# Moving 9 KB instead of 6 KB of each first row of wq, and spreading the moved rows over seven DMA engines

## The chip, the cores and the metric

The kernel runs on one core of a Trainium2 chip. A core has five compute or control engines, which the profile calls PE (TensorE, matmuls), PEld (its weight loads), DVE (VectorE), ACT (ScalarE), POOL (GpSimd) and SP (SyncE), each with its own stream of instructions, and 16 DMA engines, which carry every transfer between HBM and the on-chip memory SBUF (128 partitions). The metric is the device time of one execution in microseconds (us); the median of three runs before the change is 1315.1 us (1315.02 to 1315.15).

## The reference

One decoding step for two sequences, all in float32: a layer norm, attention of 32 query heads over a cache of 8 key/value heads with 32768 positions, an output projection, and beside it a gated MLP whose output, through a SiLU, multiplies the attention's.

```python
xn = _layernorm(x)                               # x: (2, 1, 512)
q = (xn @ wq).reshape(2, 1, 32, 128)             # wq: (512, 4096)
scores = einsum("bhqd,bhkd->bhqk", q, k) * 128 ** -0.5   # k, v: (2, 8, 32768, 128), each for 4 heads
s = (softmax(scores) @ v) @ wo                   # wo: (4096, 512)
gate, up = xn @ W_gate, xn @ W_up                # (512, 1792)
g = silu((gate * (gate > 0) * up) @ W_down)      # (1792, 512)
return x + s * g
```

The caches are 2 x 268 MB, the weights some 28 MB; everything is read once.

## The kernel before

**Staging.** SBUF holds a ring of three slots of 64 KB a partition (`SLOTS`, `SLOT` = 16384 floats). Each K or V load fills a slot: 128 partitions x 64 KB, 8 MB; for each of the 16 (sequence, KV head) groups there are two K and two V tiles. SP issues all large loads, in the order of the program (`load`, L72), and waits before each until its slot is free. DVE turns a K tile in 32 x 32 blocks in place (`turn_part`, L357), PE makes the scores (`score`, L370), then follow the maximum, the exponentials on ACT (L421), a permuting matmul (L424) and the product with V (`values`, L445). For the last two groups (L509 to L527) the order is written out by hand so that the last V tile is consumed right after it has landed. At the end the output projection `wo` comes in pieces of falling size (L533), and its products (L545, L556) end the program.

**The start.** The ring's three slots first hold weights: `wqs` (wq), `gus` (gate and up) and `wds` (W_down). The rows of wq are dealt so that partition p holds rows 4p to 4p+3; the *first row* of a partition is row 4p. wq would fill its slot with 64 KB a partition. It doesn't: the first `SHIFT` = 1536 floats (6 KB) of each of the 128 first rows are left out of the large load (L81) and are brought by loads of their own into the free end of W_down's slot (`moved`, L82). These loads have 20 rows each (`SET` = 4 x `SPREAD`, `SPREAD` = 5), arranged as 5 x 4 over the partitions, six times, and one each of 5 and of 3 rows (`REST`). They are issued from SP ahead of gate (five of them) and behind it (three), L105 to L115. `moved` has 64 partitions and `NT` = 4 columns of SHIFT floats; POOL sets it to zero beforehand (L91), since not every place is filled.

**q.** `project_q` (L224) multiplies the normed x with wq: `products(half, part)` makes chunks of 512 columns, first from `wqs` (k below `NKC` = 4), then from `moved` (k from 4 on, with `xnx`, the matching entries of x brought into the same places by small DVE copies and a transpose, L158 to L180). Two copies `qs` (L257), 8 small matmuls (L260), `turned` (L268), four matmuls with `spread` (L270) and eight copies (L281) then bring q into `qt`, which the scores read.

**The MLP.** After `project_q` come `mlp_gu(0)` and `mlp_gu(1)` (L292), `mlp_h` (L305 to L310) and `mlp_down` (L318). The calls are at L477 to L481; PE executes in this order. The slot of wq is taken by `k_0_0` when the products from `wqs` are done, that of gate and up by `k_0_1` after `mlp_gu(1)`, that of W_down and `moved` by `v_0_0` after `mlp_down` and the moved products.

**POOL** makes constants at the start: `ident`, then `qt`, `place` and others set to zero (L120 to L131), `spread` (L184), `same` (L197), `perm` (L205). It issues no DMA.

Of the kernel before, what the change touches and what calls it, by code (L numbers as in the profile page):

```python
# [8 lines left out]
F32 = mybir.dt.float32  # L9
# [4 lines left out]
P = 128  # L14
Q = 32
# [4 lines left out]
TK = P * ROWS  # L20
SLOTS = 3
ALIGN = 512
SHIFT = 1536
SPREAD = 5
WO_PIECES = (16, 8, 4, 2, 1, 1)
WO_WIDE = 28

# [2 lines left out]
def kernel(  # L30
# [12 lines left out]
    nc = tc.nc  # L43
    B, HKV, SK, DH = kc.shape
    D = x.shape[2]
# [5 lines left out]
    NKC = D // P  # L51
    FC = F // 4
    FI = F // P
# [6 lines left out]
    const = ctx.enter_context(tc.tile_pool(name="const", bufs=1))  # L60
# [7 lines left out]
    def slot(name):  # L68
        return ring.tile([P, SLOT], F32, tag="r", align_bytes=ALIGN, name=name)

    def load(dst, src):
        nc.sync.dma_start(dst, src)  # L72

    wqs, gus, wds = slot("wq"), slot("gu"), slot("wd")
    QN = wq.shape[1]
    HP = P // 2
    SET = 4 * SPREAD
    FULL = P // SET
    REST = [(FULL * SET, SPREAD), (FULL * SET + SPREAD, P - FULL * SET - SPREAD)]
    NT = FULL // 2 + 1  # L80
    load(wqs[:, : SLOT - SHIFT], wq.rearrange("(p i) n -> p (i n)", p=P)[:, SHIFT:])  # L81
    moved = wds[:HP, FI * D : FI * D + NT * SHIFT].rearrange("p (t n) -> p t n", t=NT)  # L82

    row = work.tile([P, 512], F32, tag="row", name="xp", bufs=3)
    xp = row[:32, :]
# [8 lines left out]
    def load_gu(w, src):  # L94
        load(
            gus[:, w * NKC * F : (w + 1) * NKC * F],
            src.rearrange("(p i) f -> p (i f)", p=P),
        )

    first_rows = wq.rearrange("(p i) n -> p i n", i=NKC)[:, 0, :SHIFT]  # L100

    def place_of(k):
        return slice(Q * (k % 2), Q * (k % 2) + SET), k // 2

    for k in range(FULL + len(REST)):  # L105
        if k == 5:
            load_gu(0, wg)
        part, t = place_of(k)
        if k < FULL:
            rows = first_rows[k * SET : (k + 1) * SET, :]  # L110
            load(moved[part, t, :], rows.rearrange("(b a) n -> a b n", b=4))
        else:
            at, n = REST[k - FULL]
            dst = moved[part, t, :].rearrange("(a b) n -> a b n", b=4)[:n, 0, :]
            load(dst, first_rows[at : at + n, :])  # L115
    load_gu(1, wu)
    load(wds[:, : FI * D], wd.rearrange("(p i) d -> p (i d)", p=P))
    wdt = wds[:, : FI * D].rearrange("p (i d) -> p i d", i=FI)
# [2 lines left out]
    make_identity(nc, ident)  # L121
    eps_t = const.tile([32, 1], F32, name="eps_t")
    nc.gpsimd.memset(eps_t, EPS)
    qt = const.tile([P, NG, 4, Q], F32, name="qt")
    nc.gpsimd.memset(qt, 0.0)
    place = const.tile([P, 2 * P], F32, name="place")
# [13 lines left out]
    m_ps = ps_c.tile([P, 512], F32, name="m_ps")  # L140
# [6 lines left out]
    xc, sq = xc_row[:32, :], sq_row[:32, :]  # L147
# [6 lines left out]
    nc.vector.reciprocal(st[:, 4:5], st[:, 3:4])  # L154
    nc.vector.tensor_scalar(xc, xc, st[:, 4:5], None, op0=ALU.mult)  # L155
    xnp = const.tile([P, NKC, 32], F32, name="xnp")
    xnx = const.tile([HP, NT, 32], F32, name="xnx")
    nc.vector.memset(sq, 0.0)  # L158
    xfirst = xc.rearrange("m (p i) -> m i p", i=NKC)[:, 0, :]
    for k in range(FULL + len(REST)):  # L160
        to = sq[:, k * Q : k * Q + SET].rearrange("m (a b) -> m a b", b=4)
        if k < FULL:
            cols = xfirst[:, k * SET : (k + 1) * SET]
            nc.vector.tensor_copy(to, cols.rearrange("m (b a) -> m a b", b=4))
        else:
            at, n = REST[k - FULL]
            nc.vector.tensor_copy(to[:, :n, 0], xfirst[:, at : at + n])
    xcol = xc.rearrange("b (p i) -> b i p", i=NKC)
    for i in range(NKC):
        nc.tensor.transpose(m_ps[:, i * 32 : (i + 1) * 32], xcol[:, i, :], ident[:32, :32])  # L170
    for t in range(NT):
        nc.tensor.transpose(
            m_ps[:HP, (NKC + t) * 32 : (NKC + t + 1) * 32],
            sq[:, t * HP : (t + 1) * HP],
            ident[:32, :32],
        )
    nc.vector.tensor_copy(xnp.rearrange("p k m -> p (k m)"), m_ps[:, : NKC * 32])
    nc.vector.tensor_copy(
        xnx.rearrange("p k m -> p (k m)"), m_ps[:HP, NKC * 32 : (NKC + NT) * 32]
    )  # L180

    spread = work.tile([P, 4, 4, Q], F32, tag="row", name="spread", bufs=3)
# [12 lines left out]
    n = 1  # L195
# [5 lines left out]
    for s in range(NS):  # L201
        dst = perm[:, s, :].rearrange("p (k z c h) -> p z k c h", k=4, z=2, h=REP)[:, s]
# [21 lines left out]
    def project_q():  # L224
        pick = ident.rearrange("p (c m) -> p c m", c=4)[:, :, :B]
        nq = 2 * REP * 4 * B
        def products(half, part):
            pq = S[0][half]
            for k in part:
                for c in range(4):  # L230
                    n0 = (half * 4 + c) * 512
                    cut = min(512, max(0, SHIFT - n0))
                    last = NKC + NT - 1 if cut else NKC - 1
                    i = NKC - 1 - k
                    at = cut if i == 0 else 0
                    if k < NKC and at < 512:
                        lo = i * QN + n0 - SHIFT
                        lhs, rhs, a, b = xnp[:, i, :], wqs[:, lo + at : lo + 512], at, 512
                    elif k >= NKC and cut:
                        t = k - NKC  # L240
                        lhs, rhs, a, b = xnx[:, t, :], moved[:, t, n0 : n0 + cut], 0, cut
                    else:
                        continue
                    nc.tensor.matmul(  # L244
                        pq[32 * c : 32 * c + 32, a:b],
                        lhs,
                        rhs,
                        start=(k == 0),
                        stop=(k == last),
                    )  # L250

        for part in (range(NKC), range(NKC, NKC + NT)):
            for half in range(2):
                products(half, part)
        for half in range(2):
            qs = work.tile([P, 512], F32, tag="row", name=f"qs_{half}", bufs=3)
            nc.vector.tensor_copy(qs, S[0][half])  # L257
            for h in range(REP):
                lo = (half * REP + h) * 4 * B
                nc.tensor.matmul(  # L260
                    m_ps[:, lo : lo + 4 * B],
                    qs[:, h * DH : (h + 1) * DH],
                    pick,
                    start=True,
                    stop=True,
                )
        turned = const.tile([P, nq], F32, name="turned")
        nc.vector.tensor_copy(turned, m_ps[:, :nq])  # L268
        for e in range(4):
            nc.tensor.matmul(  # L270
                pt_ps[:, e * nq : (e + 1) * nq],
                spread[:, e].rearrange("p k l -> p (k l)"),
                turned,
                start=True,
                stop=True,
            )
        qp = pt_ps[:, : 4 * nq].rearrange("p (e f h m) -> p f m e h", e=4, f=2, h=REP)
        for half in range(2):
            for kb in range(4):
                part = slice(Q * kb, Q * kb + Q)  # L280
                nc.vector.tensor_copy(  # L281
                    qt[part, half * 8 : half * 8 + 8, :, kb * REP : (kb + 1) * REP],
                    qp[part, half],
                )
# [18 lines left out]
    def mlp_h():  # L303
        g, u = gu_sb[0], gu_sb[1]
        nc.vector.scalar_tensor_tensor(  # L305
            g[:, :FC], g[:, :FC], 0.0, g[:, :FC], op0=ALU.is_gt, op1=ALU.mult
        )
        nc.vector.tensor_mul(g[:, :FC], g[:, :FC], u[:, :FC])
        ht = work.tile([P, FI, 32], F32, tag="row", name="ht", bufs=3)
        nc.vector.transpose(  # L310
            ht.rearrange("p i m -> p (i m)"), g[:, :FC].rearrange("p (f i) -> p i f", i=FI)
        )
        return ht

    def mlp_down(ht):
        for i in range(FI):
            a = i % 4
            nc.tensor.matmul(  # L318
                m_ps[32 * a : 32 * a + 32, :],
                ht[:, i, :],  # L320
                wdt[:, i, :],
                start=(i < 4),
                stop=(i >= FI - 4),
            )
        part = work.tile([P, 512], F32, tag="row", name="down", bufs=3)
        nc.vector.tensor_copy(part, m_ps)
        for c in range(4):
            nc.tensor.matmul(
                pt_ps[32 * c : 32 * c + 32, :P],
                fold,  # L330
                part[:, c * P : (c + 1) * P],
                start=True,
                stop=True,
            )
        nc.scalar.activation(gy, pt_ps[:, :P], AF.Silu)
# [117 lines left out]
    def finish_group(g):  # L453
# [11 lines left out]
        if b == B - 1:  # L465
            src = OS.pop(hk).rearrange("p b c (q i) -> p q (b c) i", q=4)
            for dq in range(4):
# [6 lines left out]
                    stop=(hk == HKV - 1 and dq == 3),  # L474
                )

    project_q()  # L477
    mlp_gu(0)
    mlp_gu(1)
    ht = mlp_h()  # L480
    mlp_down(ht)  # L481

    def load_k(g, u):
# [47 lines left out]
    i = 0  # L531
    for n in WO_PIECES:
        load(wos[:, i * D : (i + n) * D], worows[:, i * D : (i + n) * D])  # L533
# [20 lines left out]
    for i in range(WO_WIDE):  # L554
        a = i % 4
# [7 lines left out]
    part = work.tile([P, 512], F32, tag="row", name="wide", bufs=3)  # L563
# [49 lines left out]
```

## Time and profile before

| | before |
|---|---|
| median of 3 runs | 1315.1 us |
| the profiled execution: its own time | 1316.29 us |
| the profiled execution: span, first to last instruction | 1313.4 us |
| bytes read from HBM | 564.67 MB |
| rate over the span | 430 GB/s |
| PE busy | 705.6 us, 54% |
| DVE busy | 657.4 us, 50% |
| POOL busy | 11.9 us, 1% |
| granted TensorE clock, mean | 0.763 |

The span is what the profile's views cover; times in them count from its start. The DMA view, asked for a window, counts the packets that started in it and how many were "under 512 B". A load puts one packet per partition row on an engine, and behind its last one a packet of 4 bytes that reports the engine's share as done; the windows view gives for a stretch each engine's busy time, the granted clock, and the DMA engines' busy share and rate. The views don't number the DMA engines.

### The profile page before, as it was taken

How to read it: one execution, taken by the hardware profiler on the slowest of the kernel's cores; microseconds unless marked ns; L12 is line 12 of the kernel's file. 1: busy time of each engine (PE TensorE's matmuls, PEld its weight loads, DVE VectorE, ACT ScalarE, POOL GpSimd, SP SyncE). 2: the span in 40 equal slices, each digit the busy share in tenths (PEclk: the TensorE clock that was granted, in tenths of full speed). 3: DMA queues.
4: the chain of work that ended last, by engine and by line, in shares of the span. 5: the costliest groups of instructions: out<-in, count | busy, mean ns of one | idle time of the engine just before them, and what ended most of it. 6: DMA issues, size and time to landing. Idle time of an engine off the chain costs nothing.

```text
span 1313.4 us, 10129 instructions
## 1 busy us (share of the span) xinstructions
PE 705.6 (54%) x4678; PEld 198.6 (15%) x4678; DVE 657.4 (50%) x276; ACT 49.9 (4%) x133; POOL 11.9 (1%) x30
## 2 busy tenths in 40 slices
PE   3626357473645547364574636546363654726676
PEld 1201012020111102111121101111011111201121
DVE  2274471917547192653719256281835629177710
ACT  0000000000000000000000000000000000000000
POOL 3000000000000000000000000000000000000000
PEclk9757778776777867677786678879577877957798
DMA  9999999999999999999999999999999999999998
GB/s 403 444 430 434 440 434 428 438 426 441 440 426 436 430 434 438 438 425 438 430 434 441 430 430 436 430 440 436 427 438 432 432 434 438 430 438 428 422 425 353
DMA packets 11059, 565.31 MB, mean 430 GB/s; under 512 B 1280, under 2 KB 1288, under 8 KB 1802
## 3 DMA queue, kind: packets, MB, share of 16 engines
q1 hardware_dynamic: 10974, 564.67, 99.4%
q8 instruction: 36, 0.59, 0.2%
q14 instruction: 5, 0.04, 0.0%
q10 hardware_dynamic: 44, 0.01, 0.0%
HBM read 564.67 MB, written 0.00 MB: 430 GB/s over the span
## 4 chain that ended last, share of the span: by engine, by line
DMA 47%; DVE 26%; PE 25%; issue 1%; ACT 0%; SPq 0%; DVEq 0%; ACTq 0%
DMA k<-in_A_k_cache_dram 41%; DVE k L357 21%; PE o_ps L445 8%; PE s L370 7%; PE pt_ps L424 7%; DMA wo<-in_A_wo_dram 3%; DVE mx L382 3%; DVE pt L428 2%; DMA wq<-in_A_wq_dram 2%; DMA wd<-in_A_wq_dram 1%; PE s L292 1%; PE m_ps L432 0%; PE m_ps L411 0%; ACT w L421 0%; PE m_ps L400 0%
## 5 line engine op out<-in xcount | busy, mean ns | idle before, releaser
L357 DVE STREAM_TRANSPOSE k<-k 128x8192 f32<-128x8192 f32 (+2 forms) x52 | 554.8, 10672 | 136.4 <-DMA k<-in_A_k_cache_dram 136.4
L370 PE MATMUL s<-k,qt 128*32 128x512 f32 x2048 | 301.7, 749 | 479.6 <-DVE k L357 479.6
L445 PE MATMUL o_ps<-v,pt 128*16 128x512 f32 x2048 | 231.0, 609 | 7.0 <-DMA v<-in_A_v_cache_dram 7.0
L370 PEld LDWEIGHTS s<-k,qt 128*32 128x32 f32 x2048 | 71.7, 134 | 703.9 <-DVE k L357 519.1
L457 DVE SCALAR_TENSOR_TENSOR os<-o_ps,rl,mask 128x512 f32<-128x512 f32 x16 | 12.0, 750 | 226.5 <-PE o_ps L445 226.5
L424 PE MATMUL pt_ps<-w,perm 128*128 128x512 f32 x128 | 99.8, 923 | 32.7 <-ACT w L421 18.3
L421 ACT ACTIVATE w<-s,nb 128x512 f32<-128x512 f32 x64 | 43.3, 685 | 1158.2 <-DVE nb L415 1153.2
L382 DVE TENSOR_REDUCE mx<-s 128x2 f32<-128x1024 f32 x32 | 38.6, 1206 | 97.2 <-PE s L370 97.2
L445 PEld LDWEIGHTS o_ps<-v,pt 128*16 128x16 f32 x2048 | 58.2, 99 | 165.9 <-issue 156.8
L428 DVE STREAM_TRANSPOSE pt<-pt_ps 128x512 f32<-128x512 f32 x32 | 22.9, 717 | 111.9 <-PE pt_ps L424 111.9
L424 PEld LDWEIGHTS pt_ps<-w,perm 128*128 128x128 f32 x128 | 31.0, 267 | 80.7 <-issue 48.0
L469 PE MATMUL ot_ps<-os,place 128*128 128x256 f32 x64 | 16.0, 392 | 7.0 <-DVE os L457 7.0
L400 PE MATMUL m_ps<-ident,m 128*1 128x128 f32 x16 | 4.3, 270 | 24.2 <-DVE m L399 24.2
L432 PE MATMUL m_ps<-l,same 128*128 128x1 f32 x32 | 6.7, 280 | 13.5 <-DVE l L431 13.5
L469 PEld LDWEIGHTS ot_ps<-os,place 128*128 128x128 f32 x64 | 11.5, 189 | 15.6 <-DVE os L457 14.4
L421 ACT ACTIVATION_READ_ACCUMULATOR w<-s,nb 128x1 f32 x64 | 12.8, 200 | 0.0
L257 DVE COPY qs<-s 128x512 f32<-128x512 f32 x2 | 1.3, 685 | 20.7 <-PE s L244 20.7
L244 PE MATMUL s<-wq,xnp 128*32 128x512 f32 x58 | 8.7, 714 | 4.5 <-DMA wq<-in_A_wq_dram 4.5
L411 PE MATMUL m_ps<-negs,mrow 1*128 1x1 f32 x32 | 6.4, 267 | 8.3 <-DVE mrow L408 8.3
L432 PEld LDWEIGHTS m_ps<-l,same 128*128 128x128 f32 x32 | 5.4, 210 | 35.7 <-DVE l L431 35.7
L170 PE MATMUL m_ps<-ident,xc 32*128 32x32 f32 x4 | 0.7, 300 | 14.9 <-DVE xc L155 14.9
L556 PE MATMUL s<-wo,ot 128*2 128x512 f32 x56 | 6.6, 592 | 3.3 <-DMA wo<-in_A_wo_dram 3.3
(81 smaller groups left out, 95.8 us busy)
## 6 DMA issues: line engine op xcount, KB each, us to landing
v<-in_A_v_cache_dram SPq DMA_DIRECT2D x2, 4096.0 KB
wq<-in_A_wq_dram SPq DMA_DIRECT2D x1, 7424.0 KB
wo<-in_A_wo_dram SPq DMA_DIRECT2D x1, 4096.0 KB
gu<-in_B_W_gate_dram SPq DMA_DIRECT2D x1, 3584.0 KB
gu<-in_B_W_up_dram SPq DMA_DIRECT2D x1, 3584.0 KB
wd<-in_B_W_down_dram SPq DMA_DIRECT2D x1, 3584.0 KB
wo<-in_A_wo_dram SPq DMA_DIRECT2D x1, 2048.0 KB
wo<-in_A_wo_dram SPq DMA_DIRECT2D x1, 1024.0 KB
```

The lines of the kernel that those rows point to most:

```text
L244: nc.tensor.matmul(pq[32 * c : 32 * c + 32, a:b], lhs, rhs, start=(k == 0), stop=(k == last),)
L292: nc.tensor.matmul(ps[32 * c : 32 * c + 32, :FC], xnp[:, i, :], gut[:, w, i, c * FC : (c + 1) * FC], start=(i == 0), stop=(i == NKC - 1),)
L357: nc.vector.transpose(KT[t][:, part], KT[t][:, part])
L370: nc.tensor.matmul(S[u][s][Q * c : Q * c + Q, :], qt[:, g, e, :], mov[:, s, c, e], start=(e == 0), stop=(e == 3),)
L382: nc.vector.reduce_max(MX[g][:, u * NS : (u + 1) * NS], SB[u], axis=AX.X)
L421: nc.scalar.activation(w, S[u][s], AF.Exp, bias=nb, scale=SCALE, accum_out=LS[g][:, i : i + 1])
L424: nc.tensor.matmul(pt_ps, perm[:, s, :], w, start=(s == 0), stop=(s == NS - 1))
L428: nc.vector.transpose(pt.rearrange("p j m -> p (j m)"), pt_ps)
L432: nc.tensor.matmul(m_ps[:, 300:301], same.rearrange("p r h -> p (r h)"), l, start=True, stop=True)
L445: nc.tensor.matmul(o_ps[Q * a : Q * a + NC * REP], w[:, j, s * NC * REP : (s + 1) * NC * REP], v[:, s, j], start=(u == 0 and s == 0 and j ...
L457: nc.vector.scalar_tensor_tensor(OS[hk][:, b], o_ps, RL.pop(g), mask.unsqueeze(2).to_broadcast([P, NC, DH]), op0=ALU.mult, op1=ALU.mult,)
L469: nc.tensor.matmul(ot_ps.rearrange("p b c i -> p (b c) i"), place[:, lo : lo + P], src[:, dq], start=(hk == 0 and dq == 0), stop=(hk == HK ...
```

## The change

- `SHIFT` becomes 2304 floats: 9 KB of each first row leave the large load.
- The first 80 of the 128 moved rows go, as before, in loads of 20 from SP (four of them, `SETS`), over five DMA engines.
- The other 48 rows go in six loads from GpSimd (`PAIRS`), 8 rows each: four rows into one of the partitions 28 to 31, 60 and 61, four into one of 64 to 67, 96 and 97. Before, between and after them GpSimd issues small loads of x into a tile that nothing reads (`step_over`): 7 partitions, then 14 between the pairs, then 7. They have 2 x 16 bytes a partition.
- `moved` now has all 128 partitions and stays at four columns: 128 x 9216 floats. The copies that place x for it (L160) follow, and `xnx` has 128 partitions.
- gate is loaded second, ahead of all moved rows; up and W_down follow the four sets.
- `project_q` becomes two steps: PE makes the products from `wqs`, then those of gate and up, and only then the moved products and the rest of `project_q`, before `mlp_down`.

```diff
-SHIFT = 1536
+SHIFT = 2304
 SPREAD = 5
+SETS = 4
+PAIRS = 6
...
-    HP = P // 2
     SET = 4 * SPREAD
-    FULL = P // SET
-    REST = [(FULL * SET, SPREAD), (FULL * SET + SPREAD, P - FULL * SET - SPREAD)]
-    NT = FULL // 2 + 1
+    NT = (P - SETS * SET) // (2 * PAIRS)
+    PAIR = 2 * NT
+    LOW, HIGH, UNDER = 28, 64, 7
     load(wqs[:, : SLOT - SHIFT], wq.rearrange("(p i) n -> p (i n)", p=P)[:, SHIFT:])
-    moved = wds[:HP, FI * D : FI * D + NT * SHIFT].rearrange("p (t n) -> p t n", t=NT)
+    moved = wds[:, FI * D : FI * D + NT * SHIFT].rearrange("p (t n) -> p t n", t=NT)
...
-    for k in range(FULL + len(REST)):
-        if k == 5:
-            load_gu(0, wg)
+    load_gu(0, wg)
+    for k in range(SETS):
         part, t = place_of(k)
-        if k < FULL:
-            rows = first_rows[k * SET : (k + 1) * SET, :]
-            load(moved[part, t, :], rows.rearrange("(b a) n -> a b n", b=4))
-        else:
-            at, n = REST[k - FULL]
-            dst = moved[part, t, :].rearrange("(a b) n -> a b n", b=4)[:n, 0, :]
-            load(dst, first_rows[at : at + n, :])
+        rows = first_rows[k * SET : (k + 1) * SET, :]
+        load(moved[part, t, :], rows.rearrange("(b a) n -> a b n", b=4))
     load_gu(1, wu)
...
+    aside = const.tile([P, 64], F32, name="aside")
+
+    def step_over(n, m):
+        view = x[0, 0, : n * 32].rearrange("(p w) -> p w", p=n)[:, :16]
+        view = view.rearrange("p (u n) -> p u n", u=2)[:, :, :4]
+        to = aside[:n, m * 8 : m * 8 + 8].rearrange("p (u n) -> p u n", u=2)
+        nc.gpsimd.dma_start(to, view)
+
+    def pair_rows(m):
+        at = SETS * SET + m * PAIR
+        return slice(at, at + PAIR)
+
+    def low_of(m):
+        return LOW + Q * (m // 4) + m % 4
+
+    step_over(UNDER, 0)
+    for m in range(PAIRS):
+        lo = low_of(m)
+        nc.gpsimd.dma_start(
+            moved[lo : lo + HIGH - LOW + 1 : HIGH - LOW],
+            first_rows[pair_rows(m), :].rearrange("(t a) n -> a t n", a=2),
+        )
+        step_over(14 if m < PAIRS - 1 else 7, m + 1)
...
-        for part in (range(NKC), range(NKC, NKC + NT)):
-            for half in range(2):
-                products(half, part)
+        for half in range(2):
+            products(half, range(NKC))
+        yield
+        for half in range(2):
+            products(half, range(NKC, NKC + NT))
...
-    project_q()
+    steps = project_q()
+    next(steps)
     mlp_gu(0)
     mlp_gu(1)
     ht = mlp_h()
+    for _ in steps:
+        pass
     mlp_down(ht)
```

More of the change, by code (lines that the diff above doesn't have):

```diff
@@ L156 @@
     xnp = const.tile([P, NKC, 32], F32, name="xnp")
-    xnx = const.tile([HP, NT, 32], F32, name="xnx")
+    xnx = const.tile([P, NT, 32], F32, name="xnx")
     nc.vector.memset(sq, 0.0)
     xfirst = xc.rearrange("m (p i) -> m i p", i=NKC)[:, 0, :]
[L160 to L167, printed above, removed]
+    sqt = sq.rearrange("m (t p) -> m t p", t=NT)
+    for k in range(SETS):
+        part, t = place_of(k)
+        nc.vector.tensor_copy(
+            sqt[:, t, part].rearrange("m (a b) -> m a b", b=4),
+            xfirst[:, k * SET : (k + 1) * SET].rearrange("m (b a) -> m a b", b=4),
+        )
+    for m in range(PAIRS):
+        lo = low_of(m)
+        nc.vector.tensor_copy(
+            sqt[:, :, lo : lo + HIGH - LOW + 1 : HIGH - LOW],
+            xfirst[:, pair_rows(m)].rearrange("m (t a) -> m t a", a=2),
+        )
     xcol = xc.rearrange("b (p i) -> b i p", i=NKC)
@@ L172 @@
         nc.tensor.transpose(
-            m_ps[:HP, (NKC + t) * 32 : (NKC + t + 1) * 32],
-            sq[:, t * HP : (t + 1) * HP],
+            m_ps[:, (NKC + t) * 32 : (NKC + t + 1) * 32],
+            sqt[:, t, :],
             ident[:32, :32],
@@ L178 @@
     nc.vector.tensor_copy(
-        xnx.rearrange("p k m -> p (k m)"), m_ps[:HP, NKC * 32 : (NKC + NT) * 32]
+        xnx.rearrange("p k m -> p (k m)"), m_ps[:, NKC * 32 : (NKC + NT) * 32]
     )
```

## The prediction

> **What bounds the kernel now.** I read the page first: the DMA row, the queues, the chain.
>
> ```profile
> span 1313.4 us, 10129 instructions
> DMA  9999999999999999999999999999999999999998
> q1 hardware_dynamic: 10974, 564.67, 99.4%
> q8 instruction: 36, 0.59, 0.2%
> ```
>
> The 16 DMA engines are busy from end to end, almost wholly with the loads of SP's queue; all the caches and weights pass through once, and the change moves none away. The chain of waits in order of time, for the last 150 us, says what the end hangs on:
>
> ```profile
> 1199.27 32.87 DMA k<-in_A_k_cache_dram
> 1232.17 17.32 DVE k L357 x2
> 1263.14 45.24 DMA wo<-in_A_wo_dram
> 1308.43 0.62 PE s L545 x16
> ```
>
> The last weights land at 1308.4 and later, and what follows is a tail of 5 us that the change doesn't touch. A load is complete when the slowest of its engines is, so the time is that of one engine, not of the sum. What one engine moves comes from the windows view, a stretch in the middle (last columns: DMA share, GB/s):
>
> ```profile
> 700.00:719.30 19.30, 10.78 (x72) 2.66 (x76) 17.17 (x3) 0.00 (x0) 0.00 (x0) 0.64 1.00 432
> ```
>
> 432/16 = 27.0 GB/s for an engine. Now the engines against each other. Each load ends on each engine with a packet of 4 bytes, so the count "under 512 B" in a narrow window says how many engines finished a load there. The DMA view early (83.9 to 86, 86 to 89.9, 89.9 to 91 us) and late (1223.9 to 1224.6, 1224.6 to 1229.4, 1229.4 to 1232 us):
>
> ```profile
> DMA packets 27, 1.05 MB, mean 499 GB/s; under 512 B 11, under 2 KB 11, under 8 KB 11
> DMA packets 25, 1.64 MB, mean 420 GB/s; under 512 B 0, under 2 KB 0, under 8 KB 0
> DMA packets 12, 0.46 MB, mean 417 GB/s; under 512 B 5, under 2 KB 5, under 8 KB 5
> ```
>
> ```profile
> DMA packets 5, 0.13 MB, mean 187 GB/s; under 512 B 3, under 2 KB 3, under 8 KB 3
> DMA packets 28, 1.84 MB, mean 382 GB/s; under 512 B 0, under 2 KB 0, under 8 KB 0
> DMA packets 31, 1.18 MB, mean 454 GB/s; under 512 B 13, under 2 KB 13, under 8 KB 13
> ```
>
> Early, 11 engines lead and 5 follow some 6 us behind: the five that carry the moved first rows. Late, only 3 lead, by 5 to 8 us; eight others have fallen back to the five. Nothing but instruction fetch is unevenly shared in between (36 packets; the loss of about 5.5 us on each of eight engines makes 1.2 us for each of 4.5 packets, an estimate). So there are three kinds: five engines with moved rows, eight that pay for instructions, three free ones. The three use their lead for nothing:
>
> ```profile
> 1199.27 0.33 SPq L72 DMA_DIRECT2D k<-in_A_k_cache_dram  x1
> 1227.32 28.42 SPq L72 DMA_DIRECT2D v<-in_A_v_cache_dram  x4
> ```
>
> The next load after that of 1199.27 is issued at 1227.32; the three had run dry by 1224.6 and waited. One load further on (1248.4 to 1251.2) all sixteen end together:
>
> ```profile
> DMA packets 36, 1.31 MB, mean 468 GB/s; under 512 B 16, under 2 KB 16, under 8 KB 16
> ```
>
> This is the room that bytes could be put into: about 7.5 us on each of three engines.
>
> **The parts of the change.** *Less of wq in the large load.* 768 more floats of 128 first rows leave it: 8 rows x 3072 B = 24,576 B an engine, at 27.0 GB/s 0.91 us earlier for all sixteen. More than this, and what the five save, can't be won.
>
> *The five engines (0 to 4).* Before, 128 rows of 6 KB, 25 or 26 on each; after, 80 rows of 9 KB, 16 on each. The early lag of about 6.1 us over 25.6 rows is 0.24 us a row of 6 KB. A row of 9 KB costs at least 9216 B / 27.0 GB/s = 0.341 us and at most 1.5 x 0.24 = 0.36; I take 0.345, near the lower end, since a row's fixed part doesn't grow with its length. 16 x 0.345 = 5.5 us, so 0.6 us less than before.
>
> *The two engines that the GpSimd loads go to.* 48 rows, 24 on each: 24 x 0.345 = 8.3 us (8.2 to 8.6).
>
> *The small loads.* 13 GpSimd loads add 13 completions an engine, and the seven small ones 84 partition rows of two 16-byte pieces, 10.5 pieces an engine: some 24 small packets. The nearest row is that of the residual's loads, two packets in 281.0 to 281.2 us:
>
> ```profile
> q10 hardware_dynamic: 2, 0.00, 1.1%
> ```
>
> 1.1% of 16 x 0.2 us is 0.018 us a packet; 24 make 0.4 us. No load of GpSimd is in the trace, so the bounds are 0 and, with descriptors fetched for them, 1 us; I take 0.3 us on every engine.
>
> *The sum, at the load boundary of 1223.9 to 1232 us.* The eight: -0.91 + 0.3 = -0.6 us. The five: -0.6 - 0.6 = -1.2 us. The two, if they are free ones: -0.91 + 0.3 + 8.3 = +7.7 us, that is from 1223.9 to 1224.6 to 1231.6 to 1232.3. The last of the thirteen came just before 1232 (DVE's turn, which waited for it, starts at 1232.17). So the last engine is another one and comes at the same time, -0.3 to +0.4 us. That it is the same at the end follows from the dry spell: SP's issue at 1227.32 comes when the slot is free, after k tiles that land with the last engine, so it stays; engines that are now early wait there and give part of their 0.6 us back, while the two never run dry and carry their lag to the end. In the profiled execution (span 1313.4 us; its own time 1316.29 with what lies around the span, 1.2 us above the median 1315.1) the change is thus 0 within half a us, and the median stays 1315.1.
>
> *The start, which has to stay hidden.* The memset of the moved rows grows from 64 x 6144 to 128 x 9216 floats; its time goes by the columns:
>
> ```profile
> 0.74 5.21 POOL L91 MEMSET wd<- 64x6144 f32 x1 [0.29 <-POOLq L593]
> 6.43 1.81 POOL L125 MEMSET qt<- 128x2048 f32 x1
> 1.42 0.53 ACTq L89 DMA_DIRECT2D xp<-in_A_x_dram  x1
> 5.98 3.97 SPq L72 DMA_DIRECT2D wd<-in_A_wq_dram  x5
> ```
>
> 1.5 x 5.21 = 7.8 us, until 8.6. SP's four row loads wait for it, and up and W_down stand behind them; the cover is wq and, moved ahead of the wait, gate: 450,560 + 229,376 B an engine, 25 us of work. The 13 GpSimd issues stand ahead of POOL's memset of qt and all its later copies. At the 0.53 to 0.79 us an issue of ACT and SP they take 7 to 10 us, at three times that 30; the ninth also waits for the first to land. Behind them, qt is wanted first:
>
> ```profile
> 29.66 24.52 SPq L72 DMA_DIRECT2D k<-in_A_k_cache_dram  x2
> 34.86 3.63 PE L244 MATMUL s<-wd,xnx 64*32 64x512 f32 x12 [3.39 <-DMA wd<-in_A_wq_dram]
> 38.55 1.29 DVE L257 COPY qs<-s 128x512 f32<-128x512 f32 x2 [20.69 <-PE s L244]
> 45.15 4.66 PE L292 MATMUL s<-gu,xnp 128*32 128x448 f32 x32
> 45.26 2.39 DVE L281 COPY qt<-pt_ps 32x128 f32<-32x128 f32 x8 [2.12 <-PE pt_ps L270]
> 56.77 3.63 PE L318 MATMUL m_ps<-wd,ht 128*32 128x512 f32 x28 [2.98 <-DVE ht L310]
> 60.44 0.33 SPq L72 DMA_DIRECT2D v<-in_A_v_cache_dram  x1
> 71.46 17.25 DVE L357 STREAM_TRANSPOSE k<-k 128x16384 f32<-128x16384 f32 x1 [10.32 <-DMA k<-in_A_k_cache_dram]
> ```
>
> After: PE does the wq products to about 29 us, gate's, and up's when up has landed on the two loaded engines (about 46), to 49 us. Then the moved products: 20 instead of 12, in two passes as before,
>
> ```profile
> L244 PE MATMUL s<-wd,xnx 64*32 64x512 f32 x24 | 5.5, 826 | 3.4 <-DMA wd<-in_A_wq_dram 3.4
> ```
>
> so 40 rows of this group, at most 5.5 x 40/24 = 9.2 us; then q's turning (38.55 to 45.2, 6.7 us) and W_down (3.6 us): the slot of v_0_0 is free at about 68 us instead of 60.4. That costs nothing while it is before the engines end the second k tile, 83 us (the first window above). k_0_1, which needs gate's and up's slot, is issued at 49 instead of 53.9. DVE's turn of k_0_0 begins at about 71.5 as before, and the qs, qt and down copies ahead of it are through by 69. The moved rows themselves: on an engine, the residual's packets took turns with the large ones; if a row waits for one large packet each time (2.1 us of wq, 1.1 of the others), 24 rows from 12 us on are in by about 50, when PE reaches them.
>
> **Rivals.**
>
> *The rows land on engines that aren't free (slower).* No view numbers the engines, so that 7 and 8 are among the three is not to be read from the trace; it shows five engines behind where loads of 20 rows were issued, so SP's rows do go to five. If a GpSimd load of two rows takes two of the thirteen, one of these comes at 1229.4 to 1232 - 0.6 + 8.3: 1237.1 to 1239.7, or 0.6 less for one of the five. That is 5 to 7.7 us after the present last, and stays to the end: 1320 to 1323, about 1321.5. It decides from one such engine on. [...]
>
> *The pairs fall on different engines each time (the change doesn't do what it says).* 4 rows on each of twelve engines: -0.6 + 4 x 0.345 = +0.8 us on the slowest: 1315.9.
>
> *The moved rows land late.* If they come at 70 us instead of 50, v_0_0 is issued at 88 and the engines that end at 83 run dry: 5 us, 1320. For it: GpSimd issues have no row here. Against: the reserve is 15 us.
>
> *The two have more room than I think.* Then the eight set the end: 0.6 us less, 1314.5. Faster than that isn't in the change.
>
> **How the numbers follow.** About 0.2%, 2.6 us, is what a measurement of this kernel can tell from no change. The forecast has 0.66, more room 0.04 and the scattered pairs 0.07: all within 0.2%. Wrong engines have 0.15, late rows 0.04, a further 0.01 for what GpSimd loads may cost around the span; these are slower by more, 0.20. Faster by over 2.6 us has 0.03, for a mechanism that I don't see. The likeliest case's own range is 1314.0 to 1316.2; to leave out no more than 2 in 10, the range goes up to 1321.0, into the wrong-engine case.
>
> **What would show it.** Right: in the windows at about 1224 to 1232 only one engine still leads, and about 15 end together; the last completion near 1309.4; DMA packets of a GpSimd queue with 48 rows. Wrong: one or two engines ending 5 us after the rest (wrong engines); a first slice with lower GB/s and v_0_0 issued after 83 us (late rows); all engines ending a us or more earlier (my prices too high).

## The result, and the profile after

The changed kernel takes 1336.9 us (median of 5 runs, 1335.3 to 1339.0) where the kernel before took 1315.1 (5 runs): a ratio of 1.0164, 95% interval 1.015 to 1.0179. It is 21.8 us slower, far outside the forecast range of 1314.0 to 1321.0. The page of its profiled execution (its own time is 1336.91 us, so that 4.7 us lie around the span, before 2.9):

```profile
span 1332.2 us, 10176 instructions
DMA  9978999999999999999999999999999999999997
GB/s 402 438 311 346 436 421 436 433 437 437 426 441 426 439 431 431 437 435 434 425 434 437 439 433 427 431 433 439 435 433 424 439 435 433 432 435 439 412 426 331
q0 software_dynamic: 704, 0.45, 0.1%
```

A slice is 33.3 us. The third and the fourth, 67 to 133 us, have 311 and 346 GB/s, and from the fifth on the rate is that of before. So the loss lies in one place, near the start. The last line counts GpSimd's packets: 704, only 48 of them rows. The timelines of SP, PE and DVE around that place:

```profile
28.26 20.34 SPq L74 DMA_DIRECT2D k<-in_A_k_cache_dram  x2
93.81 27.29 SPq L74 DMA_DIRECT2D v<-in_A_v_cache_dram  x2
```

```profile
42.73 5.49 PE L317 MATMUL s<-gu,xnp 128*32 128x448 f32 x32 [7.18 <-DMA gu<-in_B_W_up_dram]
75.36 6.67 PE L267 MATMUL s<-wd,xnx 128*32 128x512 f32 x40 [27.15 <-DMA wd<-in_A_wq_dram]
```

```profile
93.82 0.69 DVE L351 COPY down<-m_ps 128x512 f32<-128x512 f32 x1 [2.72 <-PE m_ps L343]
94.43 25.83 DVE L382 STREAM_TRANSPOSE k<-k 128x16384 f32<-128x16384 f32 x2
```

PE is through with gate and up at 48.2 us, as forecast (49), and then idles 27.15 us, for the moved rows. All the rest is carried along: v_0_0 is issued at 93.81 instead of 60.44 (after 83 us, as the prediction's sign of late rows has it; the first slice, its other sign, stays at 402 GB/s, before 403), and DVE, which works in order, gets to k_0_0's turn at 94.43 instead of 71.46, since the copies of q and `down` stand ahead of it. Until that turn and its scores are through, k_0_0's slot isn't free for v_0_1, whose issue ends at 121.1, 27.29 us after the start of v_0_0's. What the DMA engines had to do meanwhile is in the windows view (last columns: DMA share, GB/s), first before, then after:

```profile
83.00:92.00 9.00, 3.24 (x16) 0.79 (x20) 6.95 (x2) 0.00 (x0) 0.00 (x0) 0.50 1.06 459
114.00:122.00 8.00, 3.90 (x15) 1.05 (x8) 2.65 (x6) 2.84 (x8) 0.00 (x0) 0.86 1.00 434
```

```profile
83.00:92.00 9.00, 7.81 (x44) 5.04 (x47) 3.22 (x10) 0.82 (x1) 0.00 (x0) 0.62 0.28 118
92.00:102.00 10.00, 2.19 (x24) 0.39 (x15) 8.18 (x2) 0.74 (x2) 0.00 (x0) 0.83 0.79 315
114.00:122.00 8.00, 8.00 (x72) 2.20 (x68) 7.47 (x3) 0.00 (x0) 0.00 (x0) 0.90 0.33 107
122.00:132.00 10.00, 3.46 (x28) 0.76 (x24) 8.63 (x2) 0.00 (x0) 0.00 (x0) 0.86 0.78 334
```

There are two dry spells, in which the DMA engines have nothing to carry, the first for want of v_0_0, the second of v_0_1. Idle shares times lengths: 9 x 0.72 + 10 x 0.21 = 8.6 us and 8 x 0.67 + 10 x 0.22 = 7.6, together 16.1 us of the 18.8 by which the span grew. They also level the engines, whose distances the prediction was about. The DMA view for 141.6 to 142.4 us, and for 1223.6 to 1226 and 1229 to 1232:

```profile
DMA packets 32, 1.05 MB, mean 1311 GB/s; under 512 B 16, under 2 KB 16, under 8 KB 16
DMA packets 24, 1.05 MB, mean 437 GB/s; under 512 B 8, under 2 KB 8, under 8 KB 8
DMA packets 28, 1.38 MB, mean 459 GB/s; under 512 B 7, under 2 KB 7, under 8 KB 7
```

All sixteen end v_0_1 together; by the end eight lead again and seven of the others have fallen back by some 5 us, as eight did before.

Why the rows came so late, the DMA view shows for two stretches, 56.5 to 66 and 66 to 73 us, with the packets by queue:

```profile
q1 hardware_dynamic: 73, 4.19, 101.9%
q0 software_dynamic: 51, 0.00, 0.3%
```

```profile
q1 hardware_dynamic: 55, 3.15, 103.7%
q0 software_dynamic: 35, 0.07, 2.7%
```

In the first 9.5 us GpSimd's queue moved 51 packets and no row at all: only small packets, of the loads that step and of completions. In the next 7 us come 0.07 MB, the last 8 rows of 9216 B. SP's queue is at k_0_0 there, with packets of 64 KB (4.19 MB in some 64 of its 73 packets), and the engines are full (101.9%). My reading, theory T of the experiments: every packet of GpSimd's queue, of 4 bytes too, waits for one whole packet of SP's on its engine, and the small ones stand ahead of the last rows. The single packets of the trace bear it out: on one of the two engines a row starts at 56.18 us, then come packets of 4, 8 and 4 bytes at 58.93, 61.35 and 63.77 and the next row at 66.19, each as a packet of 64 KB (2.42 us) ends; the second engine does the same 0.11 us later.

### The profile page after: what moved, and what is told of

Same layout as the page of the kernel before. It is cut to its first block, busy times and chain, and to the rows that moved or that the text cites. A ratio compares the mean times of both kernels' runs of the same rounds, so it can differ in the third digit from the quotient of the medians.

```text
span 1332.2 us, 10176 instructions
## 1 busy us (share of the span) xinstructions
PE 711.4 (53%) x4692; PEld 201.7 (15%) x4692; DVE 657.6 (49%) x278; ACT 50.2 (4%) x133; POOL 21.4 (2%) x43
## 4 chain that ended last, share of the span: by engine, by line
DMA 44%; DVE 27%; PE 26%; issue 2%; ACT 0%; POOL 0%; SPq 0%; DVEq 0%; ACTq 0%; POOLq 0%
DMA k<-in_A_k_cache_dram 35%; DVE k L382 22%; PE o_ps L470 8%; PE s L395 8%; PE pt_ps L449 7%; DMA wd<-in_A_wq_dram 5%; DMA wo<-in_A_wo_dram 4%; DVE mx L407 3%; DVE pt L453 2%; PE s L267 1%; PE m_ps L436 0%; PE m_ps L457 0%; PE m_ps L343 0%; ACT w L446 0%; PE m_ps L425 0%
## 5 line engine op out<-in xcount | busy, mean ns | idle before, releaser
L470 PE MATMUL o_ps<-v,pt 128*16 128x512 f32 x2048 | 227.2, 601 | 6.5 <-DMA v<-in_A_v_cache_dram 6.5
L449 PE MATMUL pt_ps<-w,perm 128*128 128x512 f32 x128 | 106.9, 983 | 34.0 <-ACT w L446 19.6
L267 PE MATMUL s<-wd,xnx 128*32 128x512 f32 (+1 forms) x40 | 6.7, 697 | 27.1 <-DMA wd<-in_A_wq_dram 27.1
L317 PE MATMUL s<-gu,xnp 128*32 128x448 f32 x64 | 10.0, 791 | 10.0 <-DMA gu<-in_B_W_up_dram 7.2
L267 PE MATMUL s<-wq,xnp 128*32 128x512 f32 (+1 forms) x56 | 7.6, 696 | 3.8 <-DMA wq<-in_A_wq_dram 3.8
```

The costliest lines, as they stand in the source:

```text
L267: nc.tensor.matmul(pq[32 * c : 32 * c + 32, a:b], lhs, rhs, start=(k == 0), stop=(k == last),)
L317: nc.tensor.matmul(ps[32 * c : 32 * c + 32, :FC], xnp[:, i, :], gut[:, w, i, c * FC : (c + 1) * FC], start=(i == 0), stop=(i == NKC - 1),)
L449: nc.tensor.matmul(pt_ps, perm[:, s, :], w, start=(s == 0), stop=(s == NS - 1))
L470: nc.tensor.matmul(o_ps[Q * a : Q * a + NC * REP], w[:, j, s * NC * REP : (s + 1) * NC * REP], v[:, s, j], start=(u == 0 and s == 0 and j ...
```

## The experiments

Each set is measured beside the kernel before on one chip (1315.2 to 1315.4 us). The letters in the expectations are explained in them.

**half_packets.** The changed kernel; gate, up and W_down come in two column halves each, so SP's packets beside the rows have 14 KB, not 28 KB.

```diff
+    def load_halves(dst, src):
+        n = dst.shape[1] // 2
+        load(dst[:, :n], src[:, :n])
+        load(dst[:, n:], src[:, n:])
...
-    load(wds[:, : FI * D], wd.rearrange("(p i) d -> p (i d)", p=P))
+    load_halves(wds[:, : FI * D], wd.rearrange("(p i) d -> p (i d)", p=P))
```

> The changed kernel with gate, up and W_down loaded in two halves of columns each, so that SP's packets beside the moved rows are 14 KB and not 28 KB; the GpSimd loads are as in the change. Theory T: a turn beside the weights takes 0.53 us less, the last row lands at 45 to 52 us instead of 75 us, the stream doesn't run dry, 1314.5 to 1317. Rival G (GpSimd's loads are slow by themselves, by their issue or their descriptors, whatever goes beside them): the last row still lands at 70 us or later, 1330 or more.

1315.44 us (1315.19 to 1316.04, 11 runs), ratio 1.0, interval 0.9991 to 1.0009: the whole loss is gone. PE finds the rows there, with no wait in brackets, and SP and DVE are on time:

```profile
47.59 5.32 PE L272 MATMUL s<-wd,xnx 128*32 128x512 f32 x40
```

```profile
63.32 36.93 SPq L74 DMA_DIRECT2D v<-in_A_v_cache_dram  x2
```

```profile
73.08 17.25 DVE L387 STREAM_TRANSPOSE k<-k 128x16384 f32<-128x16384 f32 x1 [9.06 <-DMA k<-in_A_k_cache_dram]
```

GpSimd's queue has the same 704 packets and 13 loads here. So neither their number by itself nor their issue costs the 21.8 us; the length of what they wait behind does. With the start mended, the balance that I forecast can be read, at the boundary of 83.5 us (windows 83.5 to 85.8, 89 to 90, 91.6 to 92.1) and at 1223.6 to 1224.6, 1224.6 to 1229 and 1229 to 1232:

```profile
DMA packets 25, 1.05 MB, mean 456 GB/s; under 512 B 9, under 2 KB 9, under 8 KB 9
DMA packets 13, 0.52 MB, mean 524 GB/s; under 512 B 5, under 2 KB 5, under 8 KB 5
DMA packets 8, 0.39 MB, mean 786 GB/s; under 512 B 2, under 2 KB 2, under 8 KB 2
DMA packets 12, 0.72 MB, mean 721 GB/s; under 512 B 1, under 2 KB 1, under 8 KB 1
DMA packets 22, 1.44 MB, mean 328 GB/s; under 512 B 0, under 2 KB 0, under 8 KB 0
DMA packets 43, 1.79 MB, mean 595 GB/s; under 512 B 15, under 2 KB 15, under 8 KB 15
```

Nine lead, five end some 5.5 us later and two some 8 us later (forecast 5.5 and 8.3). Late, one engine leads and 15 end between 1229 and 1232.

**k_halves.** The changed kernel; only k_0_0 comes in two pieces, with packets of 32 KB.

```diff
-        KT[g * NU + u] = load_tile(kc, g * NU + u, f"k_{g}_{u}")
+        pieces = 2 if g == u == 0 else 1
+        KT[g * NU + u] = load_tile(kc, g * NU + u, f"k_{g}_{u}", pieces)
```

> The changed kernel; only the load of k_0_0 is in two pieces, so that its packets have 32 KB a partition and not 64 KB. Theory T (a GpSimd packet waits its turn behind one whole packet of SP's queue, 2.41 us for 64 KB; the last load's small packets and rows stand behind k_0_0's): the stretch behind k_0_0 is half as long, the last row starts at about 64 to 66 us instead of 72.06, v_0_0 is issued at about 87, DVE's turn of k_0_0 starts at about 87.5 instead of 94.43, and since v_0_1 comes 26.6 us behind that turn's start and lands 20.6 later, the second boundary is at about 134 instead of 141.7: about 1328 us (1324 to 1331). Rival: only the packets of gate, up and W_down matter, or the rows are late for a reason that has nothing to do with the length of SP's packets: 1335 to 1338 as in the changed kernel.

1324.88 us (1323.06 to 1326.6, 4 runs), ratio 1.0073, interval 1.0058 to 1.0088.

```profile
65.48 7.81 PE L267 MATMUL s<-wd,xnx 128*32 128x512 f32 x40 [17.48 <-DMA wd<-in_A_wq_dram]
```

```profile
85.33 27.74 SPq L74 DMA_DIRECT2D v<-in_A_v_cache_dram  x2
```

PE's wait is 9.7 us shorter, and 12 us of the loss go, with nothing changed but the size of the packets of one load behind which the last rows stand. v_0_0 is issued at 85.33 (expected 87) and v_0_1 27.74 us later. The median came 3 us below the expected 1328, within its range; the four runs lie in two pairs, 1323.1 and 1323.6, 1326.2 and 1326.6, and the profile is of the slowest.

**down_first.** The changed kernel; W_down's products stand ahead of the moved ones on PE.

```diff
+    mlp_down(ht)
     for _ in steps:
         pass
-    mlp_down(ht)
```

> The changed kernel with W_down's products ahead of the moved products on PE. The rows land at 75 us as before. Theory T1 (the loss is handed on by DVE: the turn of k_0_0 stands behind the qs, qt and down copies, which wait for the rows, so the slot of k_0_0 comes 20 us late): v_0_0 is issued at about 82 us instead of 94, v_0_1 still at 115 us or later, and 1330 to 1336 stays. Theory T2 (the loss is the slot of v_0_0 alone): some 10 us less, 1323 to 1327.

1330.48 us (1329.22 to 1332.43, 4 runs), ratio 1.0115, interval 1.01 to 1.0129.

```profile
83.09 33.41 SPq L74 DMA_DIRECT2D v<-in_A_v_cache_dram  x2
```

```profile
89.93 25.84 DVE L382 STREAM_TRANSPOSE k<-k 128x16384 f32<-128x16384 f32 x2
```

v_0_0 is issued at 83.09, when the first engines end the second k tile: the first dry spell is almost gone, and yet 15 us stay. v_0_1's issue ends 33.41 us later, at 116.5, because k_0_0's turn starts at 89.93, behind q's copies. The windows 102 to 108 and 108 to 120 us:

```profile
102.00:108.00 6.00, 0.77 (x4) 0.20 (x8) 6.00 (x2) 0.00 (x0) 0.00 (x0) 0.50 0.58 251
108.00:120.00 12.00, 11.54 (x96) 2.94 (x88) 11.59 (x3) 0.00 (x0) 0.00 (x0) 0.88 0.29 98
```

6 x 0.42 + 12 x 0.71 = 11.0 us are idle here, against 7.6 in the second spell of the changed kernel. So v_0_0 alone, 10.7 us earlier, saves little: v_0_1 comes only 4.6 us earlier, and the second spell, through DVE's queue, grows.

**order_pe, steps_only, before_halves: single parts, put on the kernel before.** order_pe has only PE's new order, steps_only only the small loads, with two partitions of x in place of each load of rows, and before_halves only the halved loads.

```diff
-        for part in (range(NKC), range(NKC, NKC + NT)):
-            for half in range(2):
-                products(half, part)
+        for half in range(2):
+            products(half, range(NKC))
+        yield
+        for half in range(2):
+            products(half, range(NKC, NKC + NT))
```

> The kernel before with the new order on TensorE alone: the products from wqs, then gate's and up's, then the moved ones. The loads and their order are those of before. Theory: v_0_0 is issued about 7 us later than before's 60.44, still ahead of the 83 us at which the engines end the second k tile, so nothing runs dry: 1315.1 us (1314.8 to 1315.6). Rival (the order on TensorE costs by itself, since DVE's turn of k_0_0 comes behind the copies of q and holds up the slot of v_0_1): 1317 or more.

```diff
...
+    step_over(7, 0)
+    for m in range(6):
+        step_over(2, 7 + m)
+        step_over(14 if m < 5 else 7, m + 1)
```

> The kernel before with thirteen small GpSimd loads of x added (the seven that step, and two partitions in place of each of the six that bring rows), so without any moved row in GpSimd's queue. Theory: their packets cost the engines 0 to 0.4 us in all and nobody waits for them: 1315.3 us (1315.0 to 1315.8). Rival (thirteen GpSimd loads cost by themselves, by their issue on POOL or by their packets on all engines): 1317 or more.

> The kernel before with gate, up and W_down loaded in two column halves each, so with 14 KB packets, and nothing else. Theory: in the kernel before nothing waits for turns behind these packets that the end hangs on, so halving them alone is worth nothing: 1315.1 us (1314.8 to 1315.6). Rival (short packets are a gain of their own, and the halves in the changed kernel covered a loss with it): under 1314.

1315.94 us (10 runs, ratio 1.0004, interval 0.9995 to 1.0014), 1315.7 (10 runs, 1.0004, 0.9994 to 1.0013) and 1315.63 (10 runs, 1.0002, 0.9993 to 1.0012). No interval leaves 1 out; the medians are 0.3 to 0.7 us above before's 1315.29, order_pe's 0.3 us above the range that I gave it and before_halves's at its upper end. So neither PE's order nor the small loads nor short packets by themselves, put on the kernel before, cost or win anything that counts here.

**order_only (a miss).** The kernel before with PE's new order and with gate loaded second.

> The kernel before with only the new order: gate loaded second, the moved products made after those of gate and up; rows, sizes and queues as before. Theory T (the moved rows that GpSimd loads land late, at 75 us instead of 50, because on engines 7 and 8 each of their 44 packets waits for one large packet of SP's queue): the order by itself costs nothing, rows land by 35 us, v_0_0 is issued before 70 us, 1314.5 to 1316. Rival O (the order costs it: moved products and W_down at the end of PE's row hold the slot of v_0_0): 1325 or more.

1318.92 us (9 runs), ratio 1.0026, interval 1.0016 to 1.0036, more than expected. SP's timeline, and the windows view for 28 to 33.5 us:

```profile
5.97 24.00 SPq L72 DMA_DIRECT2D wd<-in_A_wq_dram  x8
30.02 0.41 SPq L72 DMA_DIRECT2D gu<-in_B_W_up_dram  x1
```

```profile
28.00:33.50 5.50, 5.46 (x50) 2.25 (x42) 0.00 (x0) 0.00 (x0) 0.00 (x0) 1.00 0.54 177
```

The eight row loads stretch over 24 us, up is issued only at 30.02, and the engines are half idle (0.54) until it comes. In the waits of SP's queue 7.0 us are put down to gate's landing: a row load behind gate waits for it (why it must is not shown). order_pe, with the loads in their old order, doesn't have this; the changed kernel, with four row loads from SP, doesn't either. So order_only tested something else than the order on PE.

**no_steps (a miss), halves_no_steps.** The changed kernel, and half_packets, without the seven small loads of `step_over`. I took it that the six pairs then go to twelve engines, four rows on each; no view shows which.

```diff
-    step_over(UNDER, 0)
...
-        step_over(14 if m < PAIRS - 1 else 7, m + 1)
```

> The changed kernel without the seven small loads of x that GpSimd issues; the six loads of rows stay, and go to whatever engines. Theory T: fewer packets to take turns and no more than 4 or 8 rows on an engine, the last row lands at 30 to 45 us, 1315 to 1317. If the loads of rows stayed on one pair of engines without the small loads: 24 rows and 12 to 18 small packets there, landing at 55 to 70 us, and a time between 1316 and 1330. Rival G: 1330 or more.

> half_packets without the seven small loads that step, so that the six pairs go to twelve different engines, four rows on each. By the prediction's sum 4 x 0.345 us come on the slowest engine: 1315.9 us (1315.3 to 1316.5) if no_steps lost its 5 us because its rows came late in the start. Rival (rows that come from other engines than the two cost all engines time by themselves, as the low rate between 18 and 30 us in no_steps suggests): about 1319 to 1321 again, with the first boundary about 4 us later.

1320.23 us (5 runs, ratio 1.0034, interval 1.002 to 1.0048) and 1321.7 (4 runs, 1.005, 1.0036 to 1.0064). In no_steps PE waits only 3.00 us for the rows,

```profile
55.54 5.32 PE L265 MATMUL s<-wd,xnx 128*32 128x512 f32 x40 [3.00 <-DMA wd<-in_A_wq_dram]
```

so with 480 packets in GpSimd's queue instead of 704, and, as I take it, the rows no longer all on two engines, they are nearly in time, and 16.7 us are won back; but 4 to 6 us remain over the sum's 1315.9, and short packets don't mend them. The windows 22 to 26 and 30 to 40 us of half_packets, then of halves_no_steps:

```profile
22.00:26.00 4.00, 4.00 (x36) 1.27 (x32) 0.00 (x0) 0.00 (x0) 1.11 (x2) 1.00 1.02 429
30.00:40.00 10.00, 3.61 (x28) 0.94 (x32) 1.28 (x3) 0.00 (x0) 4.74 (x22) 0.69 1.01 428
```

```profile
22.00:26.00 4.00, 3.31 (x16) 0.91 (x20) 0.00 (x0) 0.00 (x0) 0.02 (x1) 1.00 0.98 275
30.00:40.00 10.00, 4.73 (x44) 1.54 (x40) 0.00 (x0) 0.00 (x0) 0.00 (x0) 0.90 1.00 345
```

The engines are as busy (0.98 and 1.00) and move a fifth (345 against 428) to over a third less (275 against 429): the packets themselves take longer (SP's of 14 KB 0.77 us in the mean from 18 to 26 us, in half_packets 0.535) while rows come, as I take it, by other engines. The next two runs ask why.

**halves_nine, nine_ports.** half_packets with a first small load of nine partitions instead of seven, which was to bring the rows to two other engines, and then also with other partitions for the rows.

```diff
-    LOW, HIGH, UNDER = 28, 64, 7
+    LOW, HIGH, UNDER = 28, 64, 9
```

> half_packets with a first small load of 9 partitions instead of 7, so that all 48 rows go to the next two engines but one (9 and 10 if the first is engine 0). Theory: engines behind the five and not 7, 8 are of the eight that pay for instruction fetch; one of them then comes at the boundary of 1229.4 to 1232 us by 0.3 - 0.91 + 8.3 us later than before, at 1237 to 1240, and this lag stays to the end: 1320 to 1323 us, as the prediction's first rival priced it. Rival B (the eight that fall back are not fixed by number, or the fall-back comes from something else than the engine): 1315.4 us as half_packets. Rival C (any rows of GpSimd's queue outside the first two engines slow SP's packets in the start, as in halves_no_steps, whose packets of 14 KB took 724 to 807 ns instead of 535 between 18 and 26 us): packets over 600 ns there too, and the first boundary 4 us late.

```diff
-    LOW, HIGH, UNDER = 28, 64, 9
+    LOW, HIGH, UNDER = 68, 72, 9
```

> halves_nine with other places for the 48 rows and nothing else: partitions 68 to 71, 100 and 101 and 72 to 75, 104 and 105 instead of 28 to 31, 60 and 61 and 64 to 67, 96 and 97, so with LOW, HIGH = 68, 72. Theory P (an engine that writes into another engine's partitions slows that engine's packets, and the rows of halves_nine and halves_no_steps did so): SP's packets of 14 KB take 535 ns again and the rate between 30 and 40 us is 428 GB/s as in half_packets, not 336 as in halves_nine; the first boundary is at 64 us and not at 70.6. What is left is that the two engines are of the eight which pay for instruction fetch: one comes at 1237 to 1240 us at the boundary near 1230, and the time is 1320 to 1323 us, the prediction's first rival. Rival N (the partitions don't matter; the rows slow others because of the engines that carry them): 336 GB/s and about 1329 again. [...]

halves_nine: 1329.43 us (4 runs), ratio 1.0109, interval 1.0092 to 1.0126; the slow packets of rival C came (0.65 to 0.71 us in the mean for 14 KB), on top of the lag. nine_ports: 1322.73 us (4 runs), ratio 1.0058, interval 1.004 to 1.0076, within the expected 1320 to 1323. The window 30 to 40 us of each:

```profile
30.00:40.00 10.00, 4.22 (x28) 0.77 (x20) 1.29 (x3) 0.00 (x0) 6.34 (x24) 0.83 1.04 336
```

```profile
30.00:40.00 10.00, 3.66 (x38) 0.94 (x32) 1.28 (x3) 0.00 (x0) 4.75 (x22) 0.98 1.01 424
```

The same loads in the same order; only the partitions to which the rows are written differ, and the rate is whole again (424 against half_packets' 428). Nor are halves_nine's partitions slow by themselves, since half_packets writes the same ones and differs in the first small load alone. So neither the partitions nor the loads ahead set the rate by themselves; the two together do, as theory P has it. Its reason, that an engine has partitions of its own, is not shown, since no view numbers the engines; that it is also what slows no_steps and halves_no_steps is inferred, not tested. And what nine_ports still loses is the first rival's price; its late boundary, in 1228.7 to 1232.4, 1232.4 to 1237.6 and 1237.6 to 1238.7 us:

```profile
DMA packets 19, 0.33 MB, mean 89 GB/s; under 512 B 14, under 2 KB 14, under 8 KB 14
DMA packets 32, 2.10 MB, mean 403 GB/s; under 512 B 0, under 2 KB 0, under 8 KB 0
DMA packets 5, 0.15 MB, mean 134 GB/s; under 512 B 2, under 2 KB 2, under 8 KB 2
```

Two engines end at 1237.6 and later, where the rival put one at 1237.1 to 1239.7. So the rows come by other engines than in half_packets, where none ends after 1232, and yet the rate is whole: rival C's reason, the engines alone, is out.

**halves_2048.** half_packets with 8 KB of each first row instead of 9.

```diff
-SHIFT = 2304
+SHIFT = 2048
```

> The changed kernel with gate, up and W_down in column halves, as in half_packets, and 8 KB instead of 9 KB of each first row moved. Each of the two engines then gets 24 rows of 8 KB: at 0.345 us for 9 KB this is 24 x 0.307 = 7.4 us instead of 8.3; the large load has 8 x 1024 B more for each engine, +0.3 us. Theory: the balance limits, so the two come 0.6 us earlier at the boundary near 1229 to 1232 and the others 0.3 later: 0 to 0.5 us under half_packets, about 1315.1 us (1314.6 to 1315.6). Rival (something else sets the end, for instance the start): 1315.4 as half_packets or more.

1315.12 us (11 runs), before 1315.23, ratio 1.0, interval 0.999 to 1.0009. As computed it lies 0.3 us under half_packets, which is less than can be told apart. No version here beats the kernel before.

## Why the prediction was wrong

*The bound, and the three kinds of engines: right.* half_packets shows the five and the two at the forecast distances, and nine_ports that two engines end some 7 us behind the rest. A row of 6 KB takes 0.237 us in the trace of before, one of 9 KB 0.347 in that of the changed kernel (taken as 0.24 and 0.345). That the fall-back of the eight is instruction fetch is still argued, and the estimate of 1.2 us a packet was high: the 36 packets take 0.88 to 0.97 us in the trace of before, some 4.2 us for each of eight engines, against a fall-back of 5.5.

*The sum at the boundary of 1223.9 to 1232 us: right, where it can act.* One leading engine, 15 ending together, no gain: this is what half_packets measures (1315.44 against the forecast 1315.1). In the changed kernel itself the two dry spells level all engines first.

*The choice of engines: right.* The first rival's mechanism and price (1320 to 1323) are shown by nine_ports, with 1322.73; it didn't come about, since the GpSimd loads do reach free engines (15 end together in half_packets). That the engines are 0 to 4, 7 and 8, or 9 and 10, as the prediction and the expectations have them, and how `step_over`'s sizes choose them, no run shows, since no view numbers the engines. Shown is that all 48 rows come over two engines, 24 on each (the single packets of the changed kernel, in pairs 0.11 us apart), and that with nine partitions in the first small load two others carry the lag. What I lacked is that the choice has a second reason, the partitions: halves_nine, with the same loads and the rows in other partitions, costs 6.7 us more than nine_ports.

*The small loads on the engines' time: right.* steps_only can't be told from before, and the 656 small packets of the changed kernel take 5.9 us in all, 0.37 us an engine (forecast 0.3). That descriptors are fetched for them, the reason of the bound of 1 us, no run shows.

*The start: here it failed.* The memset took 7.8 us as forecast, and PE reached the moved products at 48. The step that failed is "if a row waits for one large packet each time [...] 24 rows from 12 us on are in by about 50, when PE reaches them". The rule in it held, for the residual too (in the trace of before its 256 bytes start at 281.11 us and the 4 behind them at 283.54, one packet of 64 KB, 2.42 us, later); the count was wrong. I counted 24 turns on each of the two engines, for the rows, behind packets of wq and of gate and up. The small packets, some 24 an engine in my sum on the engines' time and priced there at 0.018 us each, take turns as well, and a turn is priced by the packet that is ahead. In the whole kernel they are 656 of 704 packets; following the packets that start where another ends, I find 20 of them on each of the two engines beside the 24 rows, 44 turns and not 24: two ahead of the first row, which so comes at 17.2 us and not at 12, fifteen between the first and the last row, three behind. Without the fifteen the last row would have started at about 49 (an estimate from turns of 1.06 us and rows of 0.35); it started at 72.1. Waiting so, the last rows were still outstanding when k_0_0's packets of 64 KB came, and then 9.5 us passed without a row (56.5 to 66 us). half_packets cuts the price of a turn to half and removes the loss, k_halves cuts it behind k_0_0 alone and removes 12 us. The waits of GpSimd's issues, which I had named and not put into the 50 us, add nothing to it: from the first row to the last, 38 packets of GpSimd and 38 of SP (33 large, and 5 of 4 bytes that end a load) alternate one by one on each of the two engines, so no turn was missed for want of an issued load.

*The price of the late-rows rival: too small.* The rival, with a chance of 0.04, is what happened. It took a delay of 20 us, let it through to v_0_0 and counted one dry spell, 5 us. Measured: PE reaches the products at 75.36, and down_first, whose v_0_0 is just in time, still loses 15 us. I had seen that DVE's turn stands behind q's copies, but had noted it only as being in time; once they are late, v_0_1 is late too.

What stays open: of the 18.8 us of span some 2.7 are not in the two spells' idle shares. The profiled execution has the shortest span of the five (1332.2 to 1336.0 us) and the most time around it, 4.7 us where the others have 2.0 to 3.0; why they differ is not known, nor why k_halves' runs lie in two pairs.

## What to carry to other kernels

In this kernel a packet of another queue is priced by what it waits behind, not by its own bytes (4 bytes wait 2.42 us behind 64 KB, as a row of 9 KB does): count all packets of a load on an engine, also the small ones that carry none of its data, multiply by the packets of the queue beside them, and see which load will be there when the last ones come. Where small transfers must be in early, shorten the rows of the large loads beside them (here from 28 to 14 KB, which took away the whole 21.8 us) rather than the small transfers. And where a late operand stands ahead of other work on an engine that runs in order, price every buffer that this work frees, not only the first (with v_0_0 just in time, down_first still lost 15 us).

## What the runs showed of the hardware

- *Turns between queues go by whole packets.* The same 704 GpSimd packets cost 21.8 us beside SP packets of 28 and 64 KB, 9.6 us with k_0_0's cut to 32 KB, and nothing with those of gate, up and W_down cut to 14 KB. Packets of 4, 8 and 4 bytes and a row start one packet of 64 KB, 2.42 us, behind each other; a packet is a whole row of its load here, up to 64 KB.
- *The partitions that the rows are written to change the engines' rate.* 336 against 424 GB/s between 30 and 40 us (halves_nine, nine_ports), with the same loads and only the partitions changed; in half_packets (428), with a shorter first small load, the slow run's partitions cost nothing. Why is not shown.
- *A GpSimd load issued on POOL takes 0.54 to 0.69 us,* within the bounds that the prediction took from ACT and SP; eight go out by 13.65 us without a wait between them, the ninth waits 4.49 us for the landing of a small load, and the last load of rows was issued at 31.45 us because of the waits, which cost the rows nothing here:

```profile
13.08 0.57 POOL L137 DMA_DIRECT2D wd<-in_A_wq_dram  x1
18.13 0.54 POOL L125 DMA_DIRECT2D aside<-in_A_x_dram  x1 [4.49 <-DMA aside<-in_A_x_dram]
23.52 0.57 POOL L137 DMA_DIRECT2D wd<-in_A_wq_dram  x1 [4.85 <-DMA wd<-in_A_wq_dram]
31.45 0.57 POOL L137 DMA_DIRECT2D wd<-in_A_wq_dram  x1 [5.27 <-DMA wd<-in_A_wq_dram]
```
